# First down stage of a fused adaLN block: gate row in three column tiles, and two steps of chunk 1 moved

## The chip, the cores and the metric

The kernel runs on one core of a Trainium2 chip. The time is the device time of one execution in microseconds; before the change it is 554.07 us, the median of three runs (553.9 to 554.53). Five engines work side by side: PE (TensorE, matmuls, with its weight loads shown as PEld), DVE (VectorE), ACT (ScalarE), POOL (GpSimd) and SP (SyncE, used here for issuing loads and stores). Sixteen DMA engines move data for all of them.

## The reference

One block of a conditioned transformer in bfloat16, sequence 2048, width 576, hidden width 4608. A conditioning vector gives six rows of 576: shift, scale and gate for the attention half (sa, ca, ga) and for the feed-forward half (sb, cb, gb).

```python
mod = (silu(c) @ w_mod).reshape(1, 6, 1, -1)
sa, ca, ga, sb, cb, gb = (mod[:, i] for i in range(6))
h = layernorm(x) * (1 + ca) + sa
x = x + ga * A(h)       # 32 heads of 18; query s sees keys s, s-2, ..., s-14; softmax; @ wo
h = layernorm(x) * (1 + cb) + sb
x = x + gb * (((h @ w_gate) * (h @ w_up)) @ w_down)
```

The row gb is the same for all positions: a row of 576 numbers that has to stand on all 128 partitions to be multiplied into the result of the down product.

## The kernel before

The sequence is cut into eight chunks of 256 positions (two tiles of 128 each). The attention half goes chunk by chunk; the feed-forward half goes over five groups of tiles, 2, 4, 4, 3 and 3. A group has two stages. In the gate/up stage (`gate_up`) 36 blocks of 128 hidden columns are computed and multiplied into `hh`; in the down stage (`down`) each of the 36 blocks f is multiplied by its rows of Wd, which for each tile of the group gives a product of 512 columns (`acc`, L840) and one of 64 (`accr`, L844). The attention work of later chunks is spread over both stages as small pieces. The order on every engine is the order in which the program writes the instructions; nothing rearranges them. For the first down stage the pieces are placed by hand: the list behind `at0` gives pairs of f and piece, and a piece is written right after the products of its f.

The pieces that matter, in the first down stage, with chunk 1 and 2 in attention, chunk 3 before it:

- `gb_row` at f=0: the gate row gb. `mod_row` (L329) multiplies silu(c), repeated over 128 columns as the stationary operand (`sc_bc2`, kept in an `ln_xn` buffer, made by POOL at L1149), with the six-times-576 weights' last block (`wm5`, 512 rows, and `wm5r`, the remaining 64). So all 128 rows of the result are the same. Five products of 512 columns go into one PSUM bank, five of 64 into another; ACT casts both into `gb_bc` (L338). The weights `wm5` lie in a buffer of the pool `wd`, and the load of Wd block 2 (for f=8 to 11), issued by POOL right behind, takes that buffer over. After it POOL issues block 3, the second value load of chunk 2 (`b_ld(2, 1)`) and block 4.
- `a_ln(3)` at f=0 and `a_norm(3)` at f=3: the first layernorm of chunk 3 on DVE, into `ln_xn`. `load_x(5)` on SP follows and waits for it.
- `b_o(1)` at f=1: chunk 1's attention output transposed on PE and copied to `oT` by ACT.
- `av(n)` at f=2, 5, 9, 11, 15: the next n pieces of chunk 2's values. There are seven for each of its two tiles: four products of two offsets (L501), two adds (L508), and a last piece of two adds (L510, L512) that ends the sum in `o_sb`.
- `b_w(1, 0)` and `b_w(1, 1)` at f=4: the output projection Wo of chunk 1's two tiles, five products of 512 and five of 64 columns each (L685); DVE multiplies them by ga_bc (L687) and adds the residual. For tile 1 the 64-column products come first.
- `a_t(3)` at f=4: chunk 3's normalized input transposed (L307), evicted by ACT into `hT` (L296).
- `b_ln(1)` at f=8: the statistics of chunk 1's second layernorm on DVE.
- `qkv_block(3)` at f=10: QKV of chunk 3 (L529, values first). Between its values and its queries ACT computes the reciprocal deviation of chunk 1's norm (L267, L268), and DVE's norm (L272) comes behind.
- `turn(1)` at f=11: chunk 1's normalized rows transposed for the next group.

PSUM has eight banks; three are held by `acc`, `acc` and `accr` throughout this stage, and the tiles of the pieces take turns on the other five, each waiting until the last reader of the bank's former tile is done. In the kernel before, the transposes' `tr_pB` takes the bank of the first Wo tile's `pw`.

Of the kernel before, what the change touches and what calls it, by code (L numbers as in the profile page):

```python
# [7 lines left out]
BF = mybir.dt.bfloat16  # L8
F32 = mybir.dt.float32
# [9 lines left out]
P = 128  # L19
D = 576  # L20
DP = 640
KT = 5
KF = 4
# [12 lines left out]
FB = 4  # L36
VA = 28
VR = H - VA

MODK = (0, 4, 1, 2, 3)  # L40
QKK = (0, 1, 4, 2, 3)
# [5 lines left out]
def kernel(  # L47
# [13 lines left out]
    nc = tc.nc  # L61
# [6 lines left out]
    def pool(name, bufs, **kw):  # L68
        return ctx.enter_context(tc.tile_pool(name=name, bufs=bufs, **kw))
# [3 lines left out]
    dramp = pool("dramp", 1, space=DRAM)  # L73
    xin = pool("xin", 2)
    xres = pool("xres", 2)
    lnp = pool("lnp", 2)
# [12 lines left out]
    gup = pool("gup", 3)  # L89
    psp = pool("psp", 8, space=PSUM)  # L90

    def ps(shape, dt, name):
        return psp.tile(shape, dt, name=name, tag="bank")

    def js(j):
        return slice(j * P, (j + 1) * P)
# [9 lines left out]
    ga_bc = consts.tile([P, D], BF, name="ga_bc")  # L106
    gb_bc = consts.tile([P, D], BF, name="gb_bc")
    sc = consts.tile([P, KT], BF, name="sc")
# [7 lines left out]
    wv = wts.tile([P, KT, D], BF, name="wv")  # L116
    wo = wts.tile([P, KT, D], BF, name="wo")
    vd = dramp.tile([HALO + S, D], BF, name="vd")
    wgx_guard = tc.tile_pool(name="wgx", bufs=2)
    wgx = wgx_guard.__enter__()  # L120
    sp_guard = tc.tile_pool(name="setup", bufs=1)
# [2 lines left out]
    sc_bc = sp.tile([P, KT, P], BF, name="sc_bc")  # L124
# [56 lines left out]
    def behind(dma, load):  # L181
        tc.add_manual_dep(dma.ins, load.ins.name, SYNC, reason="value rows go first")
# [29 lines left out]
    wmC = wdp.tile([P, FB, D], BF, name="wd")  # L212
    wmCr = x1p.tile([P, D], BF, name="x1")
# [62 lines left out]
    def layernorm(src, tag):  # L276
        xn, stat, rsq, norm = ln_parts(src, tag)
        for j in range(ST):
            stat(j)

        def norms(js=range(ST)):
            for j in js:
                norm(j)
        return xn, lambda: rsq(slice(0, ST)), norms
# [13 lines left out]
    def transposed(src, dst, cols, vi, between=None, kf=KF):  # L298
        n = P * len(cols)
        pA = ps([P, 3, n], BF, "tr_pA")  # L300
        pB = ps([P, 2, n], BF, "tr_pB")
        for c, j in enumerate(cols):
            if c and between:
                between()
            for m in range(KT):
                d = pA[:, m, :] if m < 3 else pB[:, m - 3, :]
                nc.tensor.transpose(d[:, js(c)], src[:, j, m * P:(m + 1) * P], ident[:])  # L307

        def evict(on_dve=(0, 1, 2)):
            for m in range(KT):  # L310
                s = pA[:, m, :] if m < 3 else pB[:, m - 3, :]
                modulate(dst(m), s, kf if m == KF else m, vi + 1, vi, m in on_dve)
        return evict
# [10 lines left out]
        for r in (slice(0, 64), slice(64, P)):  # L324
            nc.vector.tensor_tensor(modc[r, c01, KF:KT], pm[64:P, :, KF:KT], addc[64:P, :, KF:KT], ALU.add)

    def mod_row(wm, dst, sc_bc, parts=((0, 512), (512, D))):
        outs = []
        for c0, c1 in parts:  # L329
            p_t = ps([P, c1 - c0], F32, "pa" if c0 == 0 else "pb")  # L330
            for kt in range(KT):
                nc.tensor.matmul(p_t[:], lhsT=sc_bc[:, kt, :], rhs=wm(slice(0, P), kt)[:, c0:c1],
                                 start=(kt == 0), stop=(kt == KT - 1))
            outs.append((dst[:, c0:c1], p_t))

        def evict():
            for d, p_t in outs:
                nc.scalar.copy(d, p_t[:])  # L338
        return evict


    scale = float(DH) ** -0.5
    aa, bb, h2T, x1 = {}, {}, {}, {}
# [11 lines left out]
    def a_tiles(i):  # L355
        hT = hTp.tile([P, KT, CH], BF, name="hT") if i > 1 else vshp.tile([P, KT, CH], BF, name="vsh")
        aa[i].update(hT=hT, qT=qTs[i % 2], kT=kTs[i % 2])
# [8 lines left out]
    def a_t(i, on_dve=(0, 1, 2), between=None):  # L366
        a_tiles(i)
        hT = aa[i]["hT"]
        transposed(aa[i]["xn"], lambda m: hT[:, m, :], (0, 1), 0, between, KT if i in PAIRED else KF)(on_dve)
# [33 lines left out]
    def a_v(i, j):  # L403
        hT = aa[i]["hT"]
        pv = ps([P, VA * DH], F32, "pv")
        pvr = ps([P, VR * DH], F32, "pvr")
        for kt in range(KT):
            nc.tensor.matmul(pv[:], lhsT=hT[:, kt, js(j)], rhs=wv[:, kt, 0:VA * DH], start=(kt == 0), stop=(kt == KT - 1))
        for kt in range(KT):
            nc.tensor.matmul(pvr[:], lhsT=hT[:, kt, js(j)], rhs=wv[:, kt, VA * DH:D], start=(kt == 0), stop=(kt == KT - 1))  # L410
        v_sb = vstage.tile([P, DH, H], BF, name="v_sb")[:] if i else v0(j)
        nc.scalar.copy(v_sb[:, :, 0:VA], pv[:].rearrange("p (h d) -> p d h", d=DH))
        nc.scalar.copy(v_sb[:, :, VA:H], pvr[:].rearrange("p (h d) -> p d h", d=DH))
        r0 = HALO + i * CH + j * P
        if i == 0:
            if j == 1:
                nc.gpsimd.dma_start(vd[r0 + P - HALO:r0 + P, :], o_sbs[0][P - HALO:P, j, 0:D])
            return
        nc.gpsimd.dma_start(vd[r0:r0 + P, :], v_sb.rearrange("p d h -> p (d h)"))
# [119 lines left out]
    def place_pair_rows():  # L539
        nc.gpsimd.tensor_copy(halves(wq4[64:, KF, :]), halves(wqk[64:, KF, :])[:, :, KF * P:D])  # L540
        for r in (LO, HI):
            nc.scalar.copy(modc[r, 0:2, KT], modc[0:64, 0:2, KF])
# [65 lines left out]
    def qkv_block(i, between):  # L608
        q, k, qk4, v0_, v1_ = qkv_units(i, [(0, 0, 5)])[0]
        for pair in ((v0_, v1_), (q, k), (qk4,)):  # L610
            for part in range(2):
                for unit in pair:
                    unit[part]()
            if pair[0] is v0_:
                between()
# [60 lines left out]
    def b_w(i, j):  # L676
        pw = ps([P, 512], F32, "pw")
        pwr = ps([P, 64], F32, "pwr")
        parts = [(pwr, slice(512, D)), (pw, slice(0, 512))]
        if j == 0:  # L680
            parts.reverse()
        xt = x1p.tile([P, D], BF, name="x1")
        for p_t, cs in parts:
            for m in range(KT):
                nc.tensor.matmul(p_t[:], lhsT=oT[:, m, js(j)], rhs=wo[:, m, cs], start=(m == 0), stop=(m == KT - 1))  # L685
        for p_t, cs in parts:
            nc.vector.tensor_tensor(xt[:, cs], p_t[:], ga_bc[:, cs], ALU.mult)  # L687
        nc.vector.tensor_tensor(xt[:], xt[:], x_res[i][:, j, :], ALU.add)
        x1.setdefault(i, []).append(xt)

    def b_ln(i):
        x_res.pop(i)
        bb[i]["xn"], bb[i]["rsq"], bb[i]["norm"] = layernorm(lambda j: x1[i][j], "b")
# [203 lines left out]
    wm5 = wdp.tile([P, FB, D], BF, name="wd")  # L897
    wm5r = x1p.tile([P, D], BF, name="x1")
# [203 lines left out]
    sum_j(1)  # L1102
    norm_x2(1)
    a_v(1, 0)
    ga_row = lambda part: mod_row(lambda p, k: wmC[p, k, :] if k < KF else wmCr[p, :], ga_bc, sc_bc, (part,))
    ga_out = [ga_row((0, 512))]
    a_t(2, (0, 1, 2))
    ga_out.append(ga_row((512, D)))
# [36 lines left out]
    sp_guard.__exit__(None, None, None)  # L1145
    hh0_guard = tc.tile_pool(name="hh0", bufs=1)
    hh0 = hh0_guard.__enter__().tile([P, FT, CH], BF, name="hh")
    sc_bc2 = lnp.tile([P, KT, P], BF, name="ln_xn")
    nc.gpsimd.tensor_copy(sc_bc2[:], sc[:, :, None].to_broadcast([P, KT, P]))  # L1149

    def res(i):
        return (0.0, lambda: load_res(i))
# [8 lines left out]
           4: [(1.0, nop), (1.0, early_wd)]}  # L1161
    av2 = [p for _, p in B_av(2)]
    def gb_row():
        mod_row(lambda p, k: wm5[p, k, :] if k < KF else wm5r[p, :], gb_bc, sc_bc2)()
        behind(load_wd(1), wgu_in[4])
        behind(b_ld(2, 0), wgu_in[7])
        place_pair_rows()
        load_wd(2)
        load_wd(3)
        b_ld(2, 1)  # L1170
        load_wd(4)
# [15 lines left out]
    def turn(i):  # L1187
        ht, o0 = h2_of(ST * i)
        turned.append(transposed(bb[i]["xn"], lambda m: ht[:, m, o0:o0 + CH], (0, 1), 2))
# [4 lines left out]
    def av(n):  # L1194
        for p in av2[:n]:
            p()
        del av2[:n]

    at0 = [[] for _ in range(FT - FB)]
    for f, piece in ((0, gb_row), (0, lambda: a_ln(3)), (1, lambda: b_o(1)), (2, lambda: av(2)), (3, lambda: (a_norm(3), load_x(5))),  # L1200
                     (4, lambda: b_w(1, 0)), (4, lambda: b_w(1, 1)), (4, lambda: a_t(3, ())), (5, lambda: av(2)), (8, lambda: b_ln(1)), (9, lambda: av(2)),
                     (10, lambda: qkv_block(3, bb[1]["rsq"])), (10, lambda: bb[1]["norm"]()), (11, lambda: av(5)), (11, lambda: turn(1)),
                     (15, lambda: av(3)), (15, lambda: turned.pop()()), (17, lambda: a_ln(4)), (19, lambda: b_o(2)), (22, lambda: b_w(2, 0)),
                     (22, lambda: (a_norm(4), load_x(6))), (23, lambda: last_ln(0)), (23, lambda: b_w(2, 1)), (25, lambda: a_t(4, ())),
                     (26, lambda: last_ln(1)), (30, lambda: last_norm(0)), (30, lambda: last_norm(1)), (31, lambda: b_t(2, (0,)))):
        at0[f].append(piece)
# [46 lines left out]
```

## Time and profile before

| | |
|---|---|
| median of three runs | 554.07 us |
| the profiled execution | 554.21 us |
| its span, first to last instruction | 552.5 us |
| granted TensorE clock, mean | 0.999 |
| PE busy | 542.6 us (98%) |
| DVE busy | 328.9 us (60%) |
| ACT busy | 255.5 us (46%) |
| POOL busy | 64.8 us (12%) |
| DMA, mean | 196 GB/s |

The profile is of one execution. Its time is 1.7 us longer than its span. In rows in order of time the first number is the start in us from the span's beginning, the second how long the merged instructions take, then engine, line, operation, output and input tiles, shapes and count; in square brackets stands the idle time of the engine ahead of it with what ended it. PE's records overlap, since one product starts before the last has drained; the time a product holds the engine is read from start to start. The two ends of a row of windows are in us.

### The profile page before, as it was taken

To read this page: it belongs to the slowest core of one execution; us is meant where nothing else is said; L and a number is where in the kernel's file an instruction comes from. 1 tells how busy PE (TensorE), PEld (TensorE's weight loads), DVE (VectorE), ACT (ScalarE), POOL (GpSimd) and SP (SyncE) were. 2 spreads that over 40 slices of the span, in tenths; PEclk is the share of its full clock that TensorE was granted. 3 is DMA by queue.
4 is the path that set the end of the run, shared out by engine and by line. 5 is a ranking of instruction groups with operands and counts; after the bars stand their busy time and mean duration, and the time that the engine had idled before them with its cause. 6 is when DMAs were issued, how large, how long until landed. Compare 5 with 4: busy or idle time off the path is not lost.

```text
span 552.5 us, 14851 instructions
## 1 busy us (share of the span) xinstructions
PE 542.6 (98%) x6284; PEld 326.7 (59%) x6317; DVE 328.9 (60%) x793; ACT 255.5 (46%) x606; POOL 64.8 (12%) x98
## 2 busy tenths in 40 slices
PE   8999999999999999999999999999999999999997
PEld 5887886757544465555544445556655555666564
DVE  7888899986469863547357796444537615322203
ACT  2746665545555763212655553114556511465500
POOL 3102204230000001112000100111100022200010
PEclk9999999999999999999999999999999999999999
DMA  8999999866436834436633864435595665975031
GB/s 269 281 277 311 351 306 354 273 191 229 136 116 221 275 124 142 129 94 213 222 105 126 262 223 155 129 113 146 184 289 180 209 183 188 319 225 179 1 88 32
DMA packets 70156, 108.40 MB, mean 196 GB/s; under 512 B 3690, under 2 KB 57850, under 8 KB 70090
## 3 DMA queue, kind: packets, MB, share of 16 engines
q1 hardware_dynamic: 58832, 61.50, 36.7%
q0 software_dynamic: 11168, 45.81, 25.8%
q8 instruction: 49, 0.80, 0.6%
q10 hardware_dynamic: 90, 0.15, 0.1%
q14 instruction: 17, 0.14, 0.1%
HBM read 103.00 MB, written 4.44 MB: 194 GB/s over the span
## 4 chain that ended last, share of the span: by engine, by line
PE 88%; DMA 9%; DVE 2%; issue 1%; ACT 0%; SPq 0%
PE pg L529 28%; PE pu L529 22%; PE acc L840 21%; PE pp L529 6%; PE accr L844 4%; DMA wgr<-in_B_w_gate_dram 3%; PE pw L685 2%; DMA wo<-in_A_wo_dram 2%; PE lg L448 2%; DMA wgu<-in_B_w_gate_dram 1%; DMA x_t<-in_A_x_dram 1%; DMA wmA<-in_w_mod_dram 1%; PE tr_pA L307 1%; PE tr_pB L307 0%; PE oT_pA L521 0%
## 5 line engine op out<-in xcount | busy, mean ns | idle before, releaser
L529 PE MATMUL pg<-h2T,wgu 64*128 64x512 bf16 (+2 forms) x1440 | 280.0, 333 | 0.0
L529 PE MATMUL pu<-h2T,wgu 64*128 64x512 bf16 (+2 forms) x1440 | 279.0, 333 | 0.0
L529 PEld LDWEIGHTS <-wgu 64*128 64x128 bf16 x2880 | 141.8, 94 | 102.7
L796 ACT CAST u_sb<-pu 128x512 bf16<-128x512 f32 (+2 forms) x180 | 90.2, 501 | 127.9 <-PE pg L529 124.8
L802 DVE TENSOR_TENSOR hh<-g_sb,u_sb 128x512 bf16<-128x512 bf16 (+2 forms) x180 | 66.7, 372 | 111.9 <-ACT g_sb L797 110.0
L840 PE MATMUL acc<-wd,hh 128*128 128x512 bf16 (+1 forms) x501 | 124.3, 371 | 0.2
L844 PE MATMUL accr<-wd,hh 128*128 128x64 bf16 x504 | 90.2, 193 | 1.2 <-issue 0.2
L797 ACT CAST g_sb<-pg 128x512 bf16<-128x512 f32 (+2 forms) x180 | 91.2, 507 | 0.0
L840 PEld LDWEIGHTS <-hh 128*128 128x128 bf16 x588 | 55.2, 98 | 60.4 <-issue 1.7
L529 PE MATMUL pg<-h2T,wgr 64*128 64x512 bf16 (+2 forms) x180 | 60.1, 334 | 0.2 <-DMA wgu<-in_B_w_gate_dram 0.2
L529 PE MATMUL pu<-h2T,wgr 64*128 64x512 bf16 (+2 forms) x180 | 60.2, 334 | 0.0
L166 POOL DMA_DIRECT2D wd<-in_B_w_down_dram x38 | 28.5, 751 | 229.5 <-PE accr L844 205.0
L844 PEld LDWEIGHTS <-hh 128*128 128x128 bf16 x576 | 51.8, 98 | 1.4
L501 DVE TENSOR_TENSOR vsh<-vsh,attn 128x1152 bf16<-128x1152 bf16 x56 | 40.4, 750 | 0.0
L438 DVE TENSOR_TENSOR prod<-qT,kT 128x1280 bf16<-128x1280 bf16 x46 | 36.6, 817 | 4.3 <-ACT kT L364 4.3
L529 PEld LDWEIGHTS <-wgr 64*128 64x128 bf16 x360 | 17.9, 94 | 16.1 <-issue 3.4
L687 DVE TENSOR_TENSOR x<-pw,ga_bc 128x512 bf16<-128x512 f32 x14 | 9.7, 690 | 26.8 <-PE pw L685 26.8
L427 POOL DMA_DIRECT2D vsh<-vd x14 | 12.5, 897 | 109.4 <-DVE o_sb L512 71.8
L267 ACT ACTIVATE ln_rstdb<-ln_mvb,eps 128x2 f32<-128x2 f32 (+1 forms) x10 | 3.0, 300 | 44.8 <-DVE ln_mvb L264 44.8
L294 DVE TENSOR_SCALAR h2T<-tr_pA,modc 128x128 bf16<-128x128 bf16 (+1 forms) x30 | 9.5, 370 | 23.6 <-PE tr_pA L307 23.6
L296 ACT ACTIVATE h2T<-tr_pB,modc 128x256 bf16<-128x256 bf16 (+1 forms) x18 | 8.3, 513 | 30.8 <-PE tr_pB L307 30.8
L529 PE MATMUL pp<-hT,wqk 64*128 64x256 bf16 x360 | 22.0, 269 | 0.0
(223 smaller groups left out, 565.7 us busy)
## 6 DMA issues: line engine op xcount, KB each, us to landing
wgu<-in_B_w_gate_dram SPq DMA_DIRECT2D x45, 512.0 KB, 4.4
wgu<-in_B_w_up_dram SPq DMA_DIRECT2D x45, 512.0 KB, 6.2
wd<-in_B_w_down_dram POOLq DMA_DIRECT2D x38, 576.0 KB, 4.5
vsh<-vd POOLq DMA_DIRECT2D x14, 1152.0 KB, 8.9
x_r<-in_A_x_dram SPq DMA_DIRECT2D x8, 288.0 KB, 7.4
vsh<-in_B_w_down_dram POOLq DMA_DIRECT2D x4, 576.0 KB, 9.1
out_dram<-x SPq DMA_DIRECT2D x15, 144.0 KB, 4.4
x_t<-in_A_x_dram SPq DMA_DIRECT2D x7, 288.0 KB, 5.5
```

Of the source, the lines that this page charges most:

```text
L166: return nc.gpsimd.dma_start(wb[:], B_w_down[r0:r0 + FB * P, :].rearrange("(k p) n -> p k n", p=P))
L427: return nc.gpsimd.dma_start(vsh[:].rearrange("p w d h -> p w (d h)"), vsrc)
L438: nc.vector.tensor_tensor(prod[:], aa[i]["qT"][:], aa[i]["kT"][:, :, off:off + CH], ALU.mult)
L448: nc.tensor.matmul(b["lg"][H * wl:H * (wl + 1), wq, :], lhsT=ind[:, m, :], rhs=b["prod"][4 * wq + wl][:, m, :], start=(m == 0), stop=(m == ...
L501: nc.vector.tensor_tensor(v, v, at, ALU.mult)
L529: return nc.tensor.matmul(dst, lhsT=lhs, rhs=rhs, start=first, stop=last, skip_group_check=True)
L685: nc.tensor.matmul(p_t[:], lhsT=oT[:, m, js(j)], rhs=wo[:, m, cs], start=(m == 0), stop=(m == KT - 1))
L796: nc.scalar.copy(u[:, 0:N], pu[:, 0:N])
L797: nc.scalar.copy(g[:, 0:N], pg[:, 0:N])
L802: nc.vector.tensor_tensor(hh[:, f, 0:N], g[:, 0:N], u[:, 0:N], ALU.mult)
L840: nc.tensor.matmul(a[:], lhsT=hh[:, f, js(j)], rhs=wb[:, f % FB, cs], start=(f == 0), stop=(f == FT - 1))
L844: nc.tensor.matmul(accr[:, j, :], lhsT=hh[:, f, js(j)], rhs=wb[:, f % FB, 512:D], start=(f == 0 and j == 0), stop=(f == FT - 1), skip_grou ...
```

## The change

The gate row of the feed-forward half is computed in another shape. silu(c) is repeated over 32 columns instead of 128. The 576 output columns are cut into three parts of 192, and each part is computed into its own 32 rows of one PSUM tile (rows 0 to 31, 32 to 63, 64 to 95), with 15 products of 192 columns in place of ten. ACT casts the 96 rows in one go into a tile of the pool `gup`. A DMA on SP's queue writes them to a scratch tensor in DRAM (96 rows of 384 bytes), and a second one, which waits for the first, reads one row of each part back onto all 128 partitions (384 pieces of 384 bytes) into `gb_bc`. The gate row of the attention half keeps the old shape under another name.

In the hand-written order of the first down stage, chunk 1's second Wo tile moves from f=4 to f=7 and chunk 3's transposes move from f=4 to f=7, ahead of it. The pieces of chunk 2's values are dealt out as 2, 2, 3, 4 and 3 instead of 2, 2, 2, 5 and 3, so that the last adds of its first tile stand ahead of chunk 1's norm instead of behind it. Each engine's list of instructions is otherwise the same, but the PSUM banks that later tiles take are numbered differently from here on.

```diff
+RG = 3
+RN = D // RG
...
+    gd = dramp.tile([32 * RG, RN], BF, name="gd")
...
-    def mod_row(wm, dst, sc_bc, parts=((0, 512), (512, D))):
+    def mod_row_wide(wm, dst, sc_bc, parts=((0, 512), (512, D))):
...
+    def mod_row(wm, sc32):
+        p_t = ps([P, RN], F32, "pa")
+        for kt in range(KT):
+            for g in range(RG):
+                nc.tensor.matmul(p_t[32 * g:32 * (g + 1), :], lhsT=sc32[:, kt, :], rhs=wm(kt)[:, RN * g:RN * (g + 1)],
+                                 start=(kt == 0), stop=(kt == KT - 1), skip_group_check=True)
+        return p_t
...
-    sc_bc2 = lnp.tile([P, KT, P], BF, name="ln_xn")
-    nc.gpsimd.tensor_copy(sc_bc2[:], sc[:, :, None].to_broadcast([P, KT, P]))
+    sc32 = lnp.tile([P, KT, 32], BF, name="ln_xn")
+    nc.gpsimd.tensor_copy(sc32[:], sc[:, :, None].to_broadcast([P, KT, 32]))
...
     def gb_row():
-        mod_row(lambda p, k: wm5[p, k, :] if k < KF else wm5r[p, :], gb_bc, sc_bc2)()
+        p_t = mod_row(lambda k: wm5[:, k, :] if k < KF else wm5r[:], sc32)
+        rows = gup.tile([P, RN], BF, name="gb_rows", tag="u_sb")
+        nc.scalar.copy(rows[0:32 * RG, :], p_t[0:32 * RG, :])
+        nc.sync.dma_start(gd[:], rows[0:32 * RG, :])
+        nc.sync.dma_start(gb_bc[:], bass.AP(gd.tensor, gd.offset, [[0, P], [32 * RN, RG], [1, RN]]))
         behind(load_wd(1), wgu_in[4])
         behind(b_ld(2, 0), wgu_in[7])
...
-                     (4, lambda: b_w(1, 0)), (4, lambda: b_w(1, 1)), (4, lambda: a_t(3, ())), (5, lambda: av(2)), (8, lambda: b_ln(1)), (9, lambda: av(2)),
-                     (10, lambda: qkv_block(3, bb[1]["rsq"])), (10, lambda: bb[1]["norm"]()), (11, lambda: av(5)), (11, lambda: turn(1)),
+                     (4, lambda: b_w(1, 0)), (5, lambda: av(2)), (7, lambda: a_t(3, ())), (7, lambda: b_w(1, 1)), (8, lambda: b_ln(1)), (9, lambda: av(3)),
+                     (10, lambda: qkv_block(3, bb[1]["rsq"])), (10, lambda: bb[1]["norm"]()), (11, lambda: av(4)), (11, lambda: turn(1)),
```

More of the change, by code (lines that the diff above doesn't have):

```diff
@@ L1104 @@
     a_v(1, 0)
-    ga_row = lambda part: mod_row(lambda p, k: wmC[p, k, :] if k < KF else wmCr[p, :], ga_bc, sc_bc, (part,))
+    ga_row = lambda part: mod_row_wide(lambda p, k: wmC[p, k, :] if k < KF else wmCr[p, :], ga_bc, sc_bc, (part,))
     ga_out = [ga_row((0, 512))]
```

## The prediction

> **What bounds the kernel now.** I read the page's share of busy time and its chain first, then busy time by stretch for the stage that is edited, then that stage in order of time on PE, DVE, ACT and POOL, and last the DMA view of the same stretch.
>
> ```profile
> span 552.5 us, 14851 instructions
> PE 542.6 (98%) x6284; PEld 326.7 (59%) x6317; DVE 328.9 (60%) x793; ACT 255.5 (46%) x606; POOL 64.8 (12%) x98
> PE 88%; DMA 9%; DVE 2%; issue 1%; ACT 0%; SPq 0%
> ```
>
> PE is busy for 98% of the span and holds 88% of the chain, so an edit is worth what it takes off PE's own line of work. The edited stage, the first down stage, begins at 88.4 us. In the next two rows each engine has its busy time and its count of instructions, then come the granted clock, the DMA share and GB/s.
>
> ```profile
> 88.40:98.10 9.70, 8.83 (x82) 5.14 (x83) 9.43 (x28) 5.18 (x17) 3.88 (x5) 1.00 1.08 356
> 98.10:124.00 25.90, 25.55 (x297) 16.69 (x299) 22.85 (x59) 13.37 (x38) 7.13 (x10) 1.00 0.72 226
> ```
>
> In its first 9.7 us PE is idle for 0.87 us (9.70 less 8.83) and in the other 25.9 us for 0.35. In that first stretch DVE is busy for 9.43 of 9.70 us and the 16 DMA engines are full (share 1.08, 356 GB/s). So three resources are close to their limit there, and a gain of PE has to pass the other two. PE in order of time:
>
> ```profile
> 88.91 1.03 PE L332 MATMUL pa<-wd,ln_xn 128*128 128x512 bf16 x3
> 90.14 0.38 PE L840 MATMUL acc<-wd,hh 128*128 128x512 bf16 x1
> 92.66 1.24 PE L685 MATMUL pw<-wo,oT 128*128 128x512 bf16 x5
> 95.11 0.33 PE L307 MATMUL tr_pA<-ident,ln_xn 128*128 128x128 bf16 x3
> 96.20 0.27 PE L307 MATMUL tr_pB<-ident,ln_xn 128*128 128x128 bf16 x2 [0.76 <-DVE x L687]
> 96.59 0.38 PE L840 MATMUL acc<-wd,hh 128*128 128x512 bf16 x1
> 98.03 0.19 PE L844 MATMUL accr<-wd,hh 128*128 128x64 bf16 x1
> 98.15 0.38 PE L840 MATMUL acc<-wd,hh 128*128 128x512 bf16 x1
> 99.71 2.38 PE L529 MATMUL pp<-wv,hT 64*128 64x288 bf16 x36
> 107.35 0.33 PE L307 MATMUL tr_pA<-ident,ln_xn 128*128 128x128 bf16 x3
> ```
>
> The reader sees the gate row (88.91 to 90.14, 1.23 us), the two Wo blocks of chunk 1 (92.66 to 95.11, 1.22 each), the transposes of chunk 3 with a stall in them, f=5 to 7 from 96.59, then f=8 at 98.15, chunk 3's QKV at 99.71 and chunk 1's transposes at 107.35. The step from the last product of f=7 at 98.03 to f=8 is 0.12 us long. f=8 is the first step that reads Wd block 2. That block's load is the next row, and the landing line is that of the same instruction:
>
> ```profile
> 90.57 0.76 POOL L166 DMA_DIRECT2D wd<-in_B_w_down_dram  x1 [5.76 <-PE pb L332]
> DMA to landing us min/median/max: 7.5/7.5/7.5
> ```
>
> It starts at 90.57, as soon as the gate row has released the buffer (block 2 takes the tile in which the row's weights lay), and lands 7.5 us later, at 98.07. So f=8 begins within 0.1 us of its weights' landing: PE has next to no slack against the DMA there, and what PE saves ahead of f=8 becomes a wait unless the load lands earlier too. This is the point on which the forecast turns.
>
> **The gate row.** Removed are ten products and two ACT casts; added are 15 products of 192 columns, each into 32 rows of PSUM, one cast of 192 columns, two DMAs on SP. The nearest row for the shape is the logits, 20 products into four 32-row tiles of 256 columns:
>
> ```profile
> 58.31 0.73 PE L448 MATMUL lg<-prod,ind 128*32 128x256 bf16 x20
> 58.97 0.28 PE L529 MATMUL pg<-h2T,wgr 64*128 64x256 bf16 x1
> ```
>
> They hold PE from 58.31 to 58.97, 0.66 us for five rounds of four, changes of tile shape with them. Five rounds of three at 192 columns are then 0.50 us (scaled by columns) to 0.66 (not scaled); I take 0.60. One after another they would be 15 x 192 columns; a step of 576 columns takes 0.245 (96.59 to 98.03 is six acc and five accr, so 5.9 steps), so 0.08 each and 1.22 in all. The row thus saves 0.63 us, bounded by 0.0 and 0.73.
>
> **The second Wo behind chunk 3's transposes.** With the row at 0.60, f=1 begins at 89.51 and the first Wo block at 92.03; it ends at 93.25. f=5 to 7 (six pairs, 1.47 us) now come before the transposes and end at 94.72. From there the DVE decides:
>
> ```profile
> 94.37 1.18 DVE L272 TENSOR_SCALAR ln_xn<-x_t,ln_mva,ln_rstda 128x576 bf16<-128x576 bf16 x4
> 95.46 0.69 DVE L687 TENSOR_TENSOR x<-pw,ga_bc 128x512 bf16<-128x512 f32 x1
> ```
>
> The transposes need both halves of ln_xn, the second ready at 95.55, so they end near 95.9. The five short products of the second Wo (0.14) follow. Its five long ones go into the PSUM bank that DVE clears at 95.46 + 0.69 = 96.15, so they begin at 96.20, as the stalled transposes did before, and take 1.08. PE reaches f=8 at **97.28** instead of 98.06: 0.78 us sooner, 0.87 before the old start of f=8. Nothing on DVE ahead of 96.15 waits for PE or is moved, so a cheaper or dearer gate row hardly changes 97.28: at the serial price of 1.22 the transposes would start at 95.34, still ahead of DVE.
>
> **What waits at f=8.** The load of block 2 is now released by the row's twelfth product, some 0.6 us earlier, at about 90.0. Whether it lands earlier is not shown directly. The first two rows below are the DMA view of 90.6 to 92.4 us, the next three that of 93 to 94 us (packets, MB, share of 16 engines; q0 is POOL's queue, q1 SP's), the last two the issue of gate/up's last weights and the landing line of that pair of loads, of which the up half is the later.
>
> ```profile
> q1 hardware_dynamic: 624, 0.62, 109.1%
> q0 software_dynamic: 1, 0.00, 2.7%
> ...
> DMA packets 197, 0.39 MB, mean 389 GB/s; under 512 B 7, under 2 KB 146, under 8 KB 196
> q0 software_dynamic: 50, 0.23, 60.9%
> q1 hardware_dynamic: 146, 0.14, 41.6%
> ...
> 85.58 2.24 SPq L151 DMA_DIRECT2D wgu<-in_B_w_up_dram  x1
> DMA to landing us min/median/max: 9.3/10.5/11.8
> ```
>
> For nearly 2 us after the issue q0 moves nothing while q1 uses all engines; those last weights land at 85.58 + 11.8 = 97.4, only 0.7 us before block 2. An engine that is always busy finishes the last of its backlog at the same time in whatever order it takes it, so an earlier issue moves the landing by less than 0.6, perhaps by nothing. Against that stands new traffic: 96 packets of 384 bytes written (6 for each of 16 engines), 384 read (24 each). By bytes at 356 GB/s the write costs 0.10 us and the read 0.41. By packets (197 in 1 us on 16 engines is 81 ns each) they cost 0.5 and 1.9. The read is issued only when the write has landed, and the write stands on SP's queue behind the weights that land at 97.4, so the read falls behind block 2 and only some of the write lies ahead of it. Bounds for the landing: 97.5 to 98.6. I take 0.3 us for the earlier issue less 0.2 for the write: f=8 at 98.05, **0.1 us sooner**.
>
> **What lies behind f=8.** The norm of chunk 1 goes behind two more adds:
>
> ```profile
> 103.48 1.19 DVE L272 TENSOR_SCALAR ln_xn<-x,ln_mvb,ln_rstdb 128x576 bf16<-128x576 bf16 x4 [0.96 <-ACT ln_rstdb L268]
> 104.58 0.75 DVE L510 TENSOR_TENSOR vsh<-vsh 128x1152 bf16<-128x1152 bf16 x1
> 105.37 0.46 DVE L512 TENSOR_TENSOR o_sb<-vsh 128x576 bf16<-128x576 bf16 x1
> 105.74 2.76 DVE L501 TENSOR_TENSOR vsh<-vsh,attn 128x1152 bf16<-128x1152 bf16 x4
> ```
>
> The adds (1.2 us) fill the 0.96 us in which DVE waited; the norm ends at about 104.9 instead of 104.67, and PE wants it at 107.35, so this costs nothing with 2.4 us to spare. DVE gains 0.9 us of which PE, no longer waiting for DVE here, gets nothing. DVE's next multiplication reads a value load issued at 92.06, also behind the new packets:
>
> ```profile
> DMA to landing us min/median/max: 11.8/11.8/11.8
> ```
>
> It lands at 103.9 before; delayed by up to 1.9 us it lands at 105.8, where DVE started that work anyway. Chunk 3's hT is evicted by ACT in 2.5 us (five tiles) from 96.0, ready near 98.5, against QKV at 99.6: cover 1.1 us. SP's next load, x of chunk 5, now queues behind the read's wait on the write; it is for the next gate/up stage. The row's first reader is at the end of this stage, 20 us after it lands. On POOL the broadcast copy is a quarter as wide, so three loads behind it are issued at most 0.9 us (its whole length) earlier; PE waits for none of them. The sum is -0.1 us: the profiled execution took 554.21 us (span 552.5 and 1.7 around it), 0.14 above the median 554.07, which gives 554.1 by the first and **554.0** by the median. I take the latter.
>
> **Weighed against the skill.** The trace's block 2 got hardly a packet until q1's backlog thinned. The Trainium skill, DMA: Bandwidth & Descriptors, section Queues, rings and completion order, says that each DMA engine takes turns between the queues it has work for, a packet at a time. By that rule an earlier issue would be served earlier, and the sum would be that of the first rival; 2.7% against 109.1% does not bear it out for the first 2 us, when descriptors may not have been ready. The same page's table at the top gives 512 bytes as the size below which an engine reads, modifies and writes; no run here shows that, and it speaks for the third rival.
>
> **The rivals.** First, the load lands earlier by all of its 0.6 us and the PE saving passes: f=8 at 97.3 to 97.5, 0.65 to 0.87 us off, 553.3 us. For it speaks the equal shares at 93 to 94 us, against it the saturated queues. Second, the three column tiles do not run together and the row saves nothing: PE still reaches f=8 ahead of 98.07, and the time is 554.0 all the same; the logits' 0.66 us speaks against it. Third, slower: the 384-byte packets, written and read, get in front of block 2 on its slowest DMA engine. The place is f=8, the price up to 0.5 + 1.9 us less the 0.6 of the earlier issue, so 1.2 us at two thirds, 555.3; it decides as soon as block 2 lands after 98.15. The read's wait for the write speaks against it, the full queues for it.
>
> **How the numbers follow.** Change hidden by the load (the second rival in it): 0.57, times 553.6 to 554.6. First rival: 0.23, 553.0 to 553.6, as the runs before span 0.6 us among themselves. Third: 0.20, 554.6 to 556.5. A measurement of this kernel tells 0.2%, 1.1 us, from no change: below 552.96 lies half of the first rival and a little of the rest, 0.15; above 555.18 most of the third, 0.17; 0.68 lies between. The range 553.1 to 555.1 leaves some 2 in 10 out; the likeliest case alone has 553.6 to 554.6.
>
> **What would show it.** Right: the row under 0.7 us on PE, no wait for DVE x ahead of tr_pB, DVE at the norm without its 0.96 us of idle, and a PE gap of 0.5 to 0.9 us ahead of the first product of f=8, ended by Wd block 2. Wrong: f=8 at 97.5 or earlier (load moved), at 99 or later (packets), or the row's two DMAs landing before 96 us.

## The result, and the profile after

The changed kernel takes 553.57 us (median of 22 runs, 553.11 to 554.56); the kernel before took 554.36 us in 22 runs on the same chip. The ratio is 0.9987, with a 95% interval of 0.9981 to 0.9993: 0.7 us faster by the ratio, 0.8 by the medians, a little less than the 0.2% which the prediction called the limit of telling. The time lies in the range that was given, 553.1 to 555.1, but it is the first rival's time (553.3), not that of the likeliest case (554.0), and the trace shows that it came about in another way than either.

Page of the changed kernel: span, busy time of the engines, shares of the chain.

```profile
span 551.9 us, 14866 instructions
PE 541.4 (98%) x6289; PEld 326.6 (59%) x6322; DVE 328.5 (60%) x793; ACT 255.1 (46%) x605; POOL 65.8 (12%) x98
PE 88%; DVE 2%; issue 1%; ACT 0%
```

PE's busy time is 1.2 us less, and its share of the chain is the same (the shares of this chain add up to 91%; the rest is not told in the line). The two stretches of the stage (the same ends as before, columns PE, PEld, DVE, ACT, POOL, clock, DMA share, GB/s):

```profile
88.40:98.10 9.70, 9.19 (x96) 5.21 (x93) 9.36 (x26) 5.71 (x18) 4.63 (x6) 1.00 1.07 359
98.10:124.00 25.90, 25.54 (x299) 16.82 (x300) 23.68 (x63) 12.70 (x36) 6.63 (x9) 1.00 0.74 232
```

In the first stretch PE is idle for 0.51 us in place of 0.87; DVE and the DMA engines are as full as they were. PE in order of time:

```profile
88.38 0.27 PE L540 MATMUL pg<-h2T,wgu 64*128 64x256 bf16 x1
95.08 0.34 PE L310 MATMUL tr_pA<-ident,ln_xn 128*128 128x128 bf16 x3
95.63 0.34 PE L310 MATMUL tr_pA<-ident,ln_xn 128*128 128x128 bf16 x3
96.43 1.24 PE L696 MATMUL pw<-wo,oT 128*128 128x512 bf16 x4 [0.20 <-DVE x L698]
97.50 0.38 PE L851 MATMUL acc<-wd,hh 128*128 128x512 bf16 x1
123.36 0.37 PE L540 MATMUL pg<-h2T,wgr 64*128 64x512 bf16 x1
```

f=8 starts at 97.50, straight behind the second Wo, with no gap ahead of it. What PE waits for is DVE, twice: for the second half of ln_xn (the second group of transposes at 95.63, 0.55 behind the first; the row names no releaser, but in e_late below the same step bears DVE's ln_xn) and for the clearing of the bank (0.20 us ahead of 96.43). DVE in the same stretch and at chunk 1's norm, then the load of block 2 and its landing:

```profile
94.60 1.18 DVE L275 TENSOR_SCALAR ln_xn<-x_t,ln_mva,ln_rstda 128x576 bf16<-128x576 bf16 x4
95.70 0.68 DVE L698 TENSOR_TENSOR x<-pw,ga_bc 128x512 bf16<-128x512 f32 x1
103.95 1.18 DVE L275 TENSOR_SCALAR ln_xn<-x,ln_mvb,ln_rstdb 128x576 bf16<-128x576 bf16 x4
```

```profile
89.99 0.76 POOL L169 DMA_DIRECT2D wd<-in_B_w_down_dram  x1 [4.94 <-PE pa L348]
DMA to landing us min/median/max: 6.8/6.8/6.8
```

The bank is cleared at 95.70 + 0.68 = 96.38, the long products of the second Wo follow at 96.43. Block 2 lands at 89.99 + 6.8 = 96.8, 0.7 us ahead of its first reader. Chunk 1's norm stands without the 0.96 us of idle time that it had.

The start of the program varies from one execution to the next, so the runs below are compared by their distance from one row: Z, the last product of the first gate/up stage (88.38 above; 88.21 before; 87.62 to 88.87 in all executions). "Stretch" is from Z to the first product of the next gate/up stage:

```profile
88.21 0.27 PE L529 MATMUL pg<-h2T,wgu 64*128 64x256 bf16 x1
124.00 0.37 PE L529 MATMUL pg<-h2T,wgr 64*128 64x512 bf16 x1
```

Before it is 124.00 - 88.21 = 35.79 us, after 123.36 - 88.38 = 34.98. The difference, 0.81, is as large as the gain of the medians, 0.79. Behind the stretch the program takes 428.4 to 428.6 us in every profiled execution but that of e_norm (429.3), so what is gained or lost is gained or lost inside it. The table has the same numbers for every run, in us behind Z; the landing is issue plus the duration that the trace gives.

| run | issue of block 2 | its landing | f=8 | stretch | ratio to before (95%) |
|---|---|---|---|---|---|
| before | 2.36 | 9.9 | 9.94 | 35.79 | 1 |
| e_again (before, once more) | 2.36 | 9.1 | 9.88 | 35.74 | one run |
| e_row (row alone) | 1.62 | 8.6 | 9.71 | 35.57 | 0.9997 (0.9988 to 1.0005) |
| e_norm (value pieces alone) | 2.36 | 8.3 | 9.92 | 35.78 | 0.9997 (0.9988 to 1.0006) |
| e_order (order of Wo and transposes alone) | 2.36 | 8.5 | 9.14 | 34.99 | 0.9983 (0.9973 to 0.9992) |
| after | 1.61 | 8.4 | 9.12 | 34.98 | 0.9987 (0.9981 to 0.9993) |
| e_after2 (after, once more) | 1.62 | 7.6 | 9.22 | 35.07 | 0.9985 (0.9976 to 0.9994) |
| e_pkts | 1.61 | 8.8 | 9.14 | 34.99 | 0.9986 (0.9975 to 0.9996) |
| e_late | 4.11 | 8.5 | 9.32 | 35.17 | 0.9990 (0.9980 to 0.9999) |
| e_later | 5.54 | 9.9 | 10.02 | 36.45 | one run |
| e_free | 1.61 | 8.0 | 8.53 | 34.97 | 0.9980 (0.9971 to 0.9989) |
| e_ofree | 2.36 | 8.8 | 8.92 | 35.29 | 0.9988 (0.9979 to 0.9997) |
| e_half | 1.62 | 8.1 | 8.53 | 34.49 | 0.9977 (0.9968 to 0.9986) |

### The profile page after: what moved, and what is told of

It reads as the page before. It is cut to its first block, busy times and chain, and to the rows that moved or that the text cites. A ratio compares the mean times of both kernels' runs of the same rounds, so it can differ in the third digit from the quotient of the medians.

```text
span 551.9 us, 14866 instructions
## 1 busy us (share of the span) xinstructions
PE 541.4 (98%) x6289; PEld 326.6 (59%) x6322; DVE 328.5 (60%) x793; ACT 255.1 (46%) x605; POOL 65.8 (12%) x98
## 4 chain that ended last, share of the span: by engine, by line
PE 88%; DVE 2%; issue 1%; ACT 0%
PE pg L540 28%; PE pu L540 22%; PE acc L851 21%; PE pp L540 6%; PE accr L855 4%; PE pw L696 3%; PE lg L459 2%; PE tr_pA L310 1%; PE oT_pA L532 0%; PE tr_pB L310 0%; DVE ln_xn L275 0%; DVE o_t L890 0%; PE lt L475 0%; PE pwr L696 0%; DVE ln_statsa L265 0%
```

## The experiments

Two theories stood against each other. The prediction's: f=8 starts when Wd block 2 lands, so the gain is what the landing moves. The other: f=8 is set by DVE, before the change through the stall ahead of tr_pB and after it through the bank of the second Wo, and block 2 has time to spare.

**The kernel before once more (e_again).** No edit.

> The kernel before, profiled a second time. The load of Wd block 2 landed 7.5 us after its issue in the first profile, 0.04 us ahead of f=8. Theory load (the landing bounds f=8 in the kernel before, and is where it was for a lasting reason): 7.2 to 7.8 us again, f=8 within 0.15 us behind the landing. Theory DVE (f=8 of the kernel before was set by DVE's clearing of the bank, and the landing that close to it was an accident of one execution): the landing moves by more than 0.5 us, and f=8 stays at 3.0 to 3.1 us behind the start of the second Wo tile's stalled transposes' wait, that is at 98.1 to 98.2 if the load is earlier.

One run took 554.32 us. From its trace, PE in order of time (the stall, the last product of f=7, f=8), then block 2's load with its landing line:

```profile
96.41 0.27 PE L307 MATMUL tr_pB<-ident,ln_xn 128*128 128x128 bf16 x2 [0.80 <-DVE x L687]
98.23 0.19 PE L844 MATMUL accr<-wd,hh 128*128 128x64 bf16 x1
98.26 0.38 PE L840 MATMUL acc<-wd,hh 128*128 128x512 bf16 x1
```

```profile
90.74 0.76 POOL L166 DMA_DIRECT2D wd<-in_B_w_down_dram  x1 [5.72 <-PE pb L332]
DMA to landing us min/median/max: 6.7/6.7/6.7
```

Block 2 lands at 97.4, 0.8 us ahead of f=8, and f=8 follows f=7 after 0.03 us (98.23 to 98.26), the usual step. It stands 9.88 behind Z, where it stood 9.94 in the first trace: there the load held it back by less than 0.1 us (98.03 to 98.15). The landing moved by 0.8 us and PE hardly at all, so the nearness on which the forecast turned belonged to one execution.

**The gate row alone (e_row).** The changed kernel with the pieces put back to where they were:

```diff
-(4, lambda: b_w(1, 0)), (5, lambda: av(2)), (7, lambda: a_t(3, ())), (7, lambda: b_w(1, 1)), (8, lambda: b_ln(1)), (9, lambda: av(3)),
+(4, lambda: b_w(1, 0)), (4, lambda: b_w(1, 1)), (4, lambda: a_t(3, ())), (5, lambda: av(2)), (8, lambda: b_ln(1)), (9, lambda: av(2)),
...
-(11, lambda: av(4)),
+(11, lambda: av(5)),
```

> The new gate row alone, order of the pieces as before. Both theories: the row takes 0.75 us in place of 1.23, PE stalls longer ahead of tr_pB (1.2 to 1.4 us), since DVE clears the bank at the same time as before, and f=8 begins at 98.1 to 98.3; the time is that of the kernel before, ratio 0.9995 to 1.0005. If the row's DMAs delay anything the ratio is over 1.0005.

PE of e_row in order of time, the second Wo and the transposes:

```profile
93.71 1.24 PE L696 MATMUL pw<-wo,oT 128*128 128x512 bf16 x5
95.00 0.34 PE L310 MATMUL tr_pA<-ident,ln_xn 128*128 128x128 bf16 x3
96.35 0.27 PE L310 MATMUL tr_pB<-ident,ln_xn 128*128 128x128 bf16 x2 [1.01 <-DVE x L698]
```

No difference that the runs can tell (0.9997). Of PE's 0.6 us, 0.2 went into the wait for DVE (1.01 us in place of 0.76 to 0.80) and 0.2 into the step from the second Wo to the transposes (93.71 to 95.00, while five such products take 1.08). f=8 is 0.2 us earlier, but that is not the row's: DVE's work stands 0.13 to 0.17 us earlier against Z in this execution than in the two of the kernel before, and already did ahead of the stage. From the wait's end to f=8 are 1.85 us here (96.35 to 98.20), as in e_again (96.41 to 98.26).

**The order alone (e_order).** The kernel before, with chunk 3's transposes and the second Wo moved to f=7 and nothing else:

```diff
-(4, lambda: b_w(1, 0)), (4, lambda: b_w(1, 1)), (4, lambda: a_t(3, ())), (5, lambda: av(2)),
+(4, lambda: b_w(1, 0)), (5, lambda: av(2)), (7, lambda: a_t(3, ())), (7, lambda: b_w(1, 1)),
```

> The second Wo behind chunk 3's transposes alone, gate row as before, value pieces as before. Theory DVE: PE reaches f=8 at 97.3 to 97.6 as in the changed kernel, because DVE sets that point and not the row; ratio 0.9985 to 0.9992 if the load lands by then. Theory load: the load is issued at 90.6 as before and lands at 97.9 to 98.2, so PE waits 0.4 to 0.8 us at f=8 and the ratio is 0.9995 to 1.0005. That tells whether the earlier issue, and so the row, was needed for the gain.

DVE's multiplication that clears the bank, and PE behind it:

```profile
95.44 0.68 DVE L687 TENSOR_TENSOR x<-pw,ga_bc 128x512 bf16<-128x512 f32 x1
```

```profile
96.18 1.24 PE L685 MATMUL pw<-wo,oT 128*128 128x512 bf16 x5
97.26 0.38 PE L840 MATMUL acc<-wd,hh 128*128 128x512 bf16 x1
```

This one edit carries the whole gain: stretch 34.99, as with all three. All of it lies ahead of f=8: from f=8 to the end of the stretch are 25.85 us here and in the kernel before, so the other numbering of later banks has no part in it. Block 2's load is issued as late as before the change (2.36 behind Z) and is still in time in this execution. A landing as late as the 9.9 of the first trace of the kernel before would have held f=8 back; the time of e_order (0.9983) shows no such loss. DVE's multiplication stands at 95.44, 7.32 behind Z, exactly where it stands in the changed kernel (95.70 less 88.38): DVE's work up to there does not depend on the row, and PE's arrival at f=8 follows from it.

**The value pieces alone (e_norm).** The kernel before, with `av` dealt out as 2, 2, 3, 4, 3:

```diff
-(9, lambda: av(2)),
+(9, lambda: av(3)),
...
-(11, lambda: av(5)),
+(11, lambda: av(4)),
```

> Chunk 2's value pieces dealt out as 2, 2, 3, 4, 3 alone, with the old gate row and the old order of Wo and transposes. Theory (DVE sets PE's arrival at f=8, and the norm has 2.4 us to spare): DVE stands at the norm without its 0.96 us of idle, PE gets nothing of it; from the last product of gate/up to the first one of the next gate/up (88.21 to 124.00, 35.79 us, in the kernel before) still 35.7 to 35.9; ratio to before 0.9995 to 1.0005. Rival (the 0.9 us of DVE reach PE at the next step that waits for DVE): 35.3 or less, ratio 0.999 or less.

Chunk 1's norm on DVE, and the stall on PE:

```profile
104.45 1.18 DVE L272 TENSOR_SCALAR ln_xn<-x,ln_mvb,ln_rstdb 128x576 bf16<-128x576 bf16 x4
```

```profile
96.93 0.27 PE L307 MATMUL tr_pB<-ident,ln_xn 128*128 128x128 bf16 x2 [0.84 <-DVE x L687]
```

No difference (0.9997, stretch 35.78). DVE stands at the norm without idle time, the stall is what it was, and PE gets nothing.

**Block 2's load issued later (e_late, e_later).** In the changed kernel the load is made to wait for ACT's last copy into oT (e_late) or for the last product of the first Wo tile (e_later); the three loads behind it on POOL wait too.

```diff
-        load_wd(2)
+
+    def o_then_loads():
+        behind(load_wd(2), b_o(1))
         load_wd(3)
         b_ld(2, 1)
         load_wd(4)
...
-(1, lambda: b_o(1)),
+(1, o_then_loads),
...
-(4, lambda: b_w(1, 0)),
+(4, w_then_loads),
```

The first two edits are those of e_late; e_later has the last one in their place, with `behind(load_wd(2), b_w(1, 0))`. What e_late was expected to show, and the load of block 2 and f=8 in it:

> The changed kernel with the issue of Wd block 2's load (and of the three loads behind it) held back until ACT has copied the last piece of chunk 1's oT, some 2.2 us (92.2 in place of 89.99). Theory (f=8 is set by DVE's clearing of the bank at 96.38, and block 2, landed at 96.76, has 0.74 us to spare): if the landing follows the issue it comes at 98.95, f=8 at 99.0 in place of 97.50, a PE gap of 1.5 us ahead of it; the stretch from gate/up to gate/up 36.3 in place of 34.98, ratio to before 1.001. The prediction's theory (no slack against the load): the full 2.2 us, 37.2, ratio 1.0027. Rival (the backlog of SP's queue sets the landing, whenever the load is issued): landing within 0.6 us of 96.76, f=8 at most 0.1 us later, ratio 0.9987.

```profile
92.31 0.76 POOL L169 DMA_DIRECT2D wd<-in_B_w_down_dram  x1 [7.43 <-ACT oT L535]
DMA to landing us min/median/max: 4.4/4.4/4.4
```

```profile
97.52 0.38 PE L851 MATMUL acc<-wd,hh 128*128 128x512 bf16 x1
```

The third answer came out: issued 2.3 us later, at 92.31, the load lands 4.4 us behind its issue, at 96.7, and f=8 stands at 97.52. (In this execution f=8 is 0.2 us further from Z than in the changed kernel's, because DVE's norm took longer, on which more below.) But the reason given with it, the backlog of SP's queue, is only half of it. The DMA view of the changed kernel from 90 to 92 and from 92 to 94 us, and then of e_late from 92.3 to 94 (packets, MB, share of 16 engines; q0 is POOL's queue, q1 SP's):

```profile
q1 hardware_dynamic: 695, 0.70, 109.7%
...
q1 hardware_dynamic: 436, 0.36, 57.0%
q0 software_dynamic: 82, 0.36, 50.5%
```

```profile
q0 software_dynamic: 11, 0.05, 36.0%
q1 hardware_dynamic: 149, 0.11, 20.2%
```

In the changed kernel q0 moves nothing from 90 to 92, and then shares the engines about equally from 92 to 94. In e_late q0 moves no packet from 92.3 to 93.5 either, though q1 takes only 25.8% of the engines in that time; its 11 packets lie behind 93.5. So the load has a start-up of its own, in which no backlog holds it. What follows is slower when issued early: q0 moves 0.36 MB in the 2 us from 92 to 94, beside q1, and in e_late 0.81 MB in the 2.7 us from 94 to 96.7, with nothing on q1. The Trainium skill, DMA: Bandwidth & Descriptors, section Queues, rings and completion order, has the engines take turns between queues by packets; the 57.0 against 50.5% from 92 to 94 agree with it, once a queue has packets to send.

> The changed kernel with the issue of block 2's load held back further, until the last product of chunk 1's first Wo tile (some 93.6, 3.6 us later than in the changed kernel). The run that held it back by 2.3 us landed at the same time as the changed kernel, 4.4 us behind the issue in place of 6.8. Theory now (the backlog of SP's queue sets the landing as long as the load is issued early enough): if 4.4 us is what the load needs by itself, it lands at 98.0 and f=8 begins there, 0.5 us later than in the changed kernel, with PE's idle time ended by block 2 or shown without a cause; from gate/up to gate/up 35.5. Rival (the load needs less than 4 us once the backlog is gone): landing before 97.5, no change, 34.98.

One run, 554.74 us. Through the later call the load of block 5 takes the row's buffer here and is issued first, at 89.61. PE at f=8 and at chunk 2's oT, then POOL's issue of block 2 with its landing, then DVE:

```profile
98.01 0.38 PE L852 MATMUL acc<-wd,hh 128*128 128x512 bf16 x1 [0.56 <-DMA wd<-in_B_w_down_dram]
112.31 0.56 PE L532 MATMUL oT_pA<-ident,o_sb 128*128 128x128 bf16 x7 [0.40 <-DVE o_sb L523]
```

```profile
93.53 0.75 POOL L169 DMA_DIRECT2D wd<-in_B_w_down_dram  x1 [3.16 <-PE pwr L696]
DMA to landing us min/median/max: 4.4/4.4/4.4
```

```profile
106.87 2.77 DVE L512 TENSOR_TENSOR vsh<-vsh,attn 128x1152 bf16<-128x1152 bf16 x4 [2.02 <-DMA vsh<-vd]
```

This is what the trace shows when f=8 does wait for block 2: the load lands at 93.53 + 4.4 = 97.9, f=8 follows at 98.01, and the idle time bears the load's name. In the kernel before, f=8 came as close behind the landing and had no idle time worth a mark. The late loads cost twice: f=8 is 0.9 us later, 0.2 of it from DVE's longer norm (the long products start at 96.20, 8.21 behind Z, against 8.05), and further down, since the values of chunk 2 are late too (2.02 us on DVE), another wait at o_sb. The stretch is 36.45, where 35.5 was expected.

**More small packets (e_pkts).** In the changed kernel, ahead of the row's own write:

```diff
+        nc.sync.dma_start(gb_bc[:].rearrange("p (g n) -> p g n", g=RG), w_mod[0:P, 0:RG * D].rearrange("p (g n) -> p g n", g=RG)[:, :, 0:RN])
+        for g in gx:
+            nc.sync.dma_start(g[:], rows[0:32 * RG, :])
         nc.sync.dma_start(gd[:], rows[0:32 * RG, :])
```

> The changed kernel with 672 more packets of 384 bytes ahead of the row's own: three more writes of the 96 rows to scratch tensors, and one read of 384 pieces into gb_bc, which the row's own read overwrites. That is 42 more packets for each DMA engine before block 2 lands. Theory (such a packet costs an engine some 24 ns, as in the changed kernel's trace): block 2 lands up to 1.0 us later, at 97.8, PE has 0.74 us of that covered and loses 0.3; from gate/up to gate/up 35.1 to 35.3, ratio to before 0.999. The third rival of the prediction (81 ns each): 3.4 us later, f=8 at 100.2, 37.4, ratio 1.003. Third possibility (block 2's packets take turns with these): no change, 0.9987.

No cost on PE: f=8 9.14 behind Z, stretch 34.99, ratio 0.9986. Block 2 lands 8.8 us behind Z; in the five other runs that issue it at the same place it lands at 7.6 to 8.6, so the packets cost it a few tenths or nothing, and it is still 0.3 us ahead of f=8. Not all 672 lay ahead of it: from 86.8 us to its landing at 96.7 the trace has 722 packets under 512 bytes, against 211 in e_after2 over the same stretch, so some 510 did, and q1 has 232 packets behind the landing. q1 in the last 2.2 us of that (94.5 to 96.7):

```profile
q1 hardware_dynamic: 179, 0.06, 12.0%
```

That is 0.120 x 16 x 2.2 us / 179 = 24 ns for a packet, nearly all of 384 bytes. The third rival's price, 81 ns, was taken from a microsecond in which most of the time went to much larger packets (0.23 MB of q0 in 50 packets, 0.14 MB of q1 in 146); at that price 510 packets would cost each of 16 engines 2.6 us.

**One value piece more or less ahead of the second Wo (e_free, e_ofree, e_half).** If DVE sets f=8, DVE work taken from ahead of the bank's clearing must move f=8. e_free moves both value pieces of f=2 to f=5:

```diff
-(2, lambda: av(2)),
...
-(5, lambda: av(2)),
+(5, lambda: av(4)),
```

> The changed kernel with the two value products of f=2 moved behind the first Wo tile (four at f=5 in place of two and two), which takes 1.4 us of DVE work from ahead of chunk 3's norm. Theory DVE: the bank of the first Wo is cleared 0.6 us earlier (the norm then waits for ACT), f=8 begins at 96.8 to 97.0 in place of 97.50, and the ratio to the kernel before goes from 0.9987 to 0.9975 to 0.9980. Theory load: the load lands at 96.8 or later and PE waits for it, f=8 at 97.2 to 97.5, ratio 0.9982 to 0.9990.

f=8 comes 0.59 us sooner than in the changed kernel (8.53 against 9.12), as the theory has it. But the stretch is 34.97, against 34.98: none of it is left at the end of the stage. A row of DVE and one of PE, at chunk 2's oT, show where it went:

```profile
93.24 1.19 DVE L275 TENSOR_SCALAR ln_xn<-x_t,ln_mva,ln_rstda 128x576 bf16<-128x576 bf16 x4 [0.60 <-ACT ln_rstda L271]
```

```profile
110.46 0.56 PE L532 MATMUL oT_pA<-ident,o_sb 128*128 128x128 bf16 x7 [0.23 <-DVE o_sb L523]
```

With nothing left to do ahead of the norm, DVE stands idle for 0.60 us, everything behind it is later by that, and at 110.46 PE waits for the end of chunk 2's values. The 0.9980 does not differ from the changed kernel's 0.9987 by more than the intervals.

e_ofree is the same order in the kernel with the old gate row:

```diff
-        p_t = mod_row(lambda k: wm5[:, k, :] if k < KF else wm5r[:], sc32)
...
+        mod_row(lambda p, k: wm5[p, k, :] if k < KF else wm5r[p, :], gb_bc, sc_bc2)()
```

> The run with the value pieces of f=2 moved to f=5, but with the old gate row (1.23 us on PE in place of 0.6). PE reaches f=8 about 0.6 us later than in that run: 8.9 us behind the stage's first product in place of 8.3. Theory (behind f=8 DVE's work up to o_sb at 110 sets the pace, and PE's 0.6 us were waited away there, since the stretch from gate/up to gate/up was 34.97 with them and 34.98 without): no difference, 34.9 to 35.1, ratio to before 0.998 to 0.999, so the row is worth nothing in any order. Rival (the row pays once DVE is out of the way ahead of f=8): 35.5, ratio 0.9991 to 0.9995, 0.5 us above the other.

The norm on DVE in e_ofree:

```profile
93.99 1.49 DVE L272 TENSOR_SCALAR ln_xn<-x_t,ln_mva,ln_rstda 128x576 bf16<-128x576 bf16 x4 [0.60 <-ACT ln_rstda L268]
```

Neither expectation is met: the stretch is 35.29, 0.32 more than e_free, between 35.1 and 35.5. PE waits for o_sb here too (0.24 us, 0.23 in e_free), and 0.3 us is also what the norm took longer here (1.49 in place of 1.19). DVE's rows settle which it is: the norm starts 5.63 behind Z here and 5.62 in e_free, and from its start to that of the last add into o_sb DVE goes without a pause in both, 17.02 us here and 16.71 there, with the other rows equally long. So the 0.32 is the lengthened norm; the row puts f=8 0.39 us later, and PE waits that away at o_sb. The times do not part the two runs (0.9988 and 0.9980, the intervals overlap).

e_half moves one of the two pieces:

```diff
-(2, lambda: av(2)),
+(2, lambda: av(1)),
...
-(5, lambda: av(2)),
+(5, lambda: av(3)),
```

> The changed kernel with one of the two value pieces of f=2 moved to f=5 (1, 3, 3, 4, 3 in place of 2, 2, 3, 4, 3). Theory (ahead of f=8 PE waits for DVE by some 0.5 us, and behind it DVE's work up to o_sb follows without a pause 0.85 us ahead of PE; moving both pieces opened a pause of 0.60 us on DVE, which came back as a wait for o_sb): with one piece of 0.7 us moved DVE has no pause, the transposes come 0.3 to 0.5 us earlier and nothing is given back; from gate/up to gate/up 34.5 to 34.7 us in place of 34.98 (and 34.97 with both moved), ratio to before 0.998. Rival (DVE is the bound all the way to o_sb and whatever PE gains ahead of f=8 is waited away behind it): 34.9 to 35.0, ratio 0.9987, PE waiting 0.2 us or more for o_sb.

The norm on DVE, and PE at f=8, at chunk 2's oT and at the next gate/up stage:

```profile
93.78 1.18 DVE L275 TENSOR_SCALAR ln_xn<-x_t,ln_mva,ln_rstda 128x576 bf16<-128x576 bf16 x4
```

```profile
88.15 0.27 PE L540 MATMUL pg<-h2T,wgu 64*128 64x256 bf16 x1
96.68 0.38 PE L851 MATMUL acc<-wd,hh 128*128 128x512 bf16 x1
110.46 0.61 PE L532 MATMUL oT_pA<-ident,o_sb 128*128 128x128 bf16 x8
122.64 0.37 PE L540 MATMUL pg<-h2T,wgr 64*128 64x512 bf16 x1
```

DVE has no pause at the norm, f=8 is as early as in e_free, PE does not wait for o_sb, and the stretch is 122.64 - 88.15 = 34.49. It has the lowest time of these kernels, 552.88 us (ratio 0.9977, 0.9968 to 0.9986), though by the times alone it can't be told from e_free (0.9980).

**The changed kernel once more (e_after2).** No edit.

> The changed kernel once more, to stand beside the run with one piece moved and to see how far the landing of Wd block 2 varies from one execution to the next. Theory: ratio 0.9987, from gate/up to gate/up 34.9 to 35.1, block 2 landing between 8.0 and 9.9 us behind the last product of gate/up (9.9 and 9.1 in two executions of the kernel before, 8.4 in one of the changed kernel), f=8 at 9.1 behind it. The prediction's theory: f=8 comes with the landing, wherever that is.

Beside e_half on the same chip the changed kernel took 553.46 (0.9985): 0.6 us between them by the medians, 0.58 by the stretches (35.07 and 34.49), while the two intervals still overlap. In this second execution block 2 landed 0.8 us sooner behind Z than in the first, sooner than the expected 8.0 to 9.9, and f=8 did not follow it (9.22 and 9.12).

## Why the prediction was right and wrong

- **The gate row, 0.63 us saved.** Right. In e_half, where all records are there, PE has

```profile
88.82 0.19 PE L855 MATMUL accr<-wd,hh 128*128 128x64 bf16 x1
88.94 0.51 PE L348 MATMUL pa<-wd,ln_xn 128*32 128x192 bf16 x12
89.47 0.39 PE L851 MATMUL acc<-wd,hh 128*128 128x512 bf16 x1
```

  A product of 64 columns holds PE for 0.03 us (98.23 to 98.26 above), so from 88.85 to 89.47 the row (its last three products are a row of their own, at 89.28) takes 0.62 us against the 0.60 predicted; the three tiles do run together, and the second rival is out.
- **PE's arrival at f=8, 97.28, set by DVE and independent of the row.** Right, and it was what came out: 9.07 behind Z predicted (97.28 less 88.21), 9.12 measured, 9.14 with the old row.
- **f=8 then waits for block 2 until 98.05.** Wrong; this is the step that failed. None of the gap of 0.5 to 0.9 us that was to show it stands ahead of f=8 in the changed kernel, which starts at 97.50, at the bound that was named as a sign of being wrong. The prediction read "f=8 begins within 0.1 us of its weights' landing" as "PE has next to no slack against the DMA there". The second execution of the same kernel had 0.8 us of slack, and among the five executions with the load issued 2.36 behind Z that one landing is the latest, 9.9 against 8.3 to 9.1. The row of f=8 named no wait for the load, while that of e_later, where the load is late, does.
- **An earlier issue moves the landing by 0.3 of its 0.6 us.** Not shown either way: issued 2.36 us behind Z the load lands at 8.3 to 9.9, issued at 1.62 at 7.6 to 8.8, and issued at 4.11 at 8.5. In the mean that is 8.9 and 8.3 for the first two, 0.6 apart for issues 0.74 apart, but either group spreads by more than 1 us. The prediction's thought that the landing hardly depends on the issue holds for e_late, though not only for its reason, the full engines; it was wrong to take one landing for its place.
- **The first rival.** Its time (553.3) and its f=8 (97.3 to 97.5) came out, its reason did not: with the old row and the late issue (e_order) the gain is the same. So the chance of 0.23 was too low because the case in which the load does not bind at all was not among the rivals.
- **The third rival, 384-byte packets ahead of block 2.** Out: 672 more of them, some 510 ahead of block 2's landing, cost PE nothing. The term that was mis-sized is the 81 ns; 24 were measured.
- **The norm behind the adds, free.** Right: e_norm 0.9997, and the norm ends at 103.95 + 1.18 = 105.1, where 104.9 was said, in an execution that began 0.2 us later.

The measured 0.13% lies within the 0.2% that had the chance of 0.68; that PE's saving would pass had 0.23. That the time fell into the range 553.1 to 555.1 is luck as far as the mechanism goes: the gain forecast was 0.1 us, the gain measured 0.8, and the range was wide enough for both. The chances also had a slip of their own: the first rival was given 553.0 to 553.6, all of it above 552.96, and yet half of it was counted below.

## What to carry to other kernels

A start that follows a landing by 0.1 us is not yet a bound: look whether idle time ahead of it is named after the load, and whether the two stay together in a second execution. Profile the unchanged kernel twice before a forecast rests on such a nearness. Where PE's arrival is set by another engine's line of work, make the sum along that engine first: here it gave f=8 to 0.05 us, and neither a row half as dear nor an earlier load changed it. Work taken off such an engine must leave it busy: by the traces, one execution each, one piece moved brought 0.5 us, and two pieces opened a pause which gave all of it back.

## What the runs showed of the hardware

Two things were not expected. The landing of one and the same load, in a stretch in which the DMA engines are full, varies by 0.8 us from execution to execution of one kernel, in both kernels that were profiled twice.

And DVE's norm of chunk 3, four instructions which take 1.18 or 1.19 us together in eight of the thirteen executions, took 1.36 to 1.62 in the other five, one instruction being lengthened to 533 to 743 ns. In each of the five, POOL was issuing a load over that instruction, and it ended within 0.15 us of the issue's end. In e_later the norm ends at 95.93, its last instruction being the long one, and POOL's issue at 95.92:

```profile
94.31 1.62 DVE L275 TENSOR_SCALAR ln_xn<-x_t,ln_mva,ln_rstda 128x576 bf16<-128x576 bf16 x4
```

```profile
95.03 0.89 POOL L438 DMA_DIRECT2D vsh<-vd  x1
```

The Trainium skill, SBUF — State Buffer, section SBUF: two separate sides, says that DVE and GpSimd share a pair of ports, and that a GpSimd instruction or a DVE instruction in a two-port mode, whichever starts first, holds it until its end while the other engine waits. The five cases agree with that in kind, though no row tells the mode in which the norm ran. But other instructions of the norm ran at their usual length under an issue (the last ones in the changed kernel, with POOL's issue at 95.38), and no run here takes the issues away, so the cause is argued and not shown.
